# A fused attention and gated-expert kernel: the first loads of k in halves, and the second heads of q on another load queue

## The chip, the cores and the metric

The kernel runs on one core of one Trainium2 chip. The metric is the device time of one execution in microseconds (us), as the median over several runs. A core has a matrix engine (PE, with its weight loads shown apart as PEld), a vector engine (DVE), a scalar engine (ACT), a general engine (POOL, also called GpSimd) and a sync engine (SP) that here only starts transfers. Each engine works through its own instructions in the order in which the program lists them. Transfers between the main memory (HBM) and the on-chip memory are started by SP, ACT and POOL, each with its own queue, and carried by 16 DMA engines that all queues share.

## The reference

Grouped-query attention over 8 batches, 16 query heads, 4 key heads, 384 positions and 64 elements a head, then a two-level gate over 16 experts and the chosen expert's two matrix products for each token.

```
scores = scale * np.matmul(q, k.transpose(0, 1, 3, 2))      # k, v repeated 4 times over heads
attn = softmax(scores)
x = matmul(attn, v)  ->  (3072 tokens, 1024)
g_idx = argmax(x @ w_group);  e_idx = argmax(x @ w_expert[g_idx])
out[token] = g_w * e_w * (relu(x @ w1[g, e]) @ w2[g, e])
```

## The kernel before

The kernel goes through the batches b = 0 to 7. For a batch, attention is cut into NU = 24 units: 4 key heads g (each with its four query heads, held as KG = 2 pairs) times NC = 6 key slices c. The class `Attn` lists the work of a unit: `score(u)` makes four matmuls of q and k into a score tile (L310) and lets ACT take the exponential into a tile e (L316); `pv(u)` multiplies e with v in fp32 (L329); `tail(u)` adds e tiles in pairs on POOL (L336, for c = 1 and 3) and reduces them on DVE (L343) into the softmax's sums. `run` calls `score(u + 2)`, `pv(u)`, `tail(u)` in that order, and after some units the pieces of other work that a table lists by hand (L731 to 745): transposes of q and k, sums, scaling, the gate, the fetch of expert weights. The schedule is manual: the order of the program is the order on each engine. The experts of batch b - 1 (L622, L633) are interleaved with the attention of batch b.

Only the first batch's start is touched here. Before any score can be computed, k and q of batch 0 must be loaded, cast to bf16 and transposed. For later batches this is done by transposing transfers; for batch 0 it is done on PE, with an identity matrix, to be quick:

- SP's queue begins with the first two key heads' rows of k (`k0f[:, 0]`, L157), then the two partition halves of v for key head 0 (`load_v0(0, 1)`, L150), the two halves of v for key heads 1 to 3 (`load_v0(1, Hkv)`, L150 again), the other two heads of k (`k0f[:, 1]`, L173), and v of batch 1 (L107). After these come the transposing transfers of batch 1 (L131, L133, L125), which wait for loads of POOL's queue.
- ACT's queue begins with the two tiles of query heads that key head 0 needs (`q0f[:, 0]` and `q0f[:, 1]`, L159, called q0 and q1 below), then the two gate matrices (L161, L162). ACT then loads its table for the exponential and runs a dummy exponential (L164).
- POOL's queue loads the rest of q of batch 0 with a cast (L170), and k and q of batch 1 (L97, L102).

`first_scores` (L266) orders the start on PE, DVE and ACT. PE runs four small and six large matmuls of ones as filling (L277, L273), DVE casts k (L279), ACT casts q0 (L280), DVE casts q1 (L281). `first_k` transposes the six slices of k twice each (12 transposes, L254) and ACT copies them out to kT (L245). `first_q` transposes q0 and q1 (three each, L262) and DVE copies them out to qT (L247). Two more fillings (L273) follow on PE. Then DVE makes three small index tiles (`index_constants`, L217 to 219), PE computes the first two scores (`at[0].start()`, L676), and `gate_matrix_a` transposes the gate matrices (L225) with two copies on DVE (L227, L231).

Later pieces that the prediction speaks of, all in the first batch or the second: POOL casts the second half of k (`cast_k`, L288) after unit 3 and then adds up v for a guess of the gate (`sum_v`, L467 to 469) after unit 4; DVE makes the inverse sums (L419), spreads them (L426) and scales (L435). PSUM tiles come in two rings, "s" and "o", of two tiles each; "x" is the "o" tile that is not the current one.

Of the kernel before, what the change touches and what calls it, by code (L numbers as in the profile page):

```python
# [18 lines left out]
def kernel(  # L19
# [11 lines left out]
    nc = tc.nc  # L31
    P = 128
    B, Hq, S, D = q.shape
# [7 lines left out]
    KG = KQ // Hkv  # L41
# [3 lines left out]
    H2 = P // 2  # L45
    NC = S // H2
# [22 lines left out]
    def ps_tile(which, shape=None, dtype=F32):  # L69
        if which == "x":  # L70
            which = f"o{1 - turn['o']}"
        else:
            turn[which] = 1 - turn[which]
            which += str(turn[which])
        return psum.tile(shape or [P, 2, 512], dtype, name="ps_" + which)
# [3 lines left out]
    NK = Hkv // 2 * NC  # L79
    k16, qraw, vraw, qT, kT = {}, {}, {}, {}, {}  # L80

    def rows(x):
        return x.rearrange("h (p c) d -> (h p) (c d)", c=NC).rearrange("(a p) n -> p a n", p=P)
# [26 lines left out]
    def new_qT(b):  # L110
        qT[b] = xpool.tile([P, KQ * SC, P], BF16, name="qT")

    def new_kT(b):
        kT[b] = xpool.tile([P, NK, P], BF16, name="kT")
# [26 lines left out]
    q0f = stage[:, :4 * NQ].bitcast(F32).rearrange("p (a n) -> p a n", n=NQ)  # L141
    k0f = stage[:, 4 * NQ:8 * NQ].bitcast(F32).rearrange("p (a n) -> p a n", n=NQ)
# [2 lines left out]
    vraw[0] = vpool.tile([P, Hkv, NC * D], F32, name="v_raw")  # L145
    wraw = stage[:NE // 2 * 5, 16 * NQ:16 * NQ + 2 * Eg * P].bitcast(F32)

    def load_v0(g0, g1):
        for r in range(2):
            nc.sync.dma_start(out=vraw[0][r * H2:(r + 1) * H2, g0:g1],  # L150
                              in_=v[0, g0:g1].rearrange("h (p c) d -> p h (c d)", c=NC))

    onesb = cpool.tile([P, 4 * P], BF16)
    ones1 = cpool.tile([P, P], BF16)
    nc.vector.memset(ones1, 1.0)
    nc.vector.memset(onesb, 1.0)
    nc.sync.dma_start(out=k0f[:, 0], in_=rows(k[0])[:, 0])  # L157
    for m in range(KG):
        nc.scalar.dma_start(out=q0f[:, m], in_=rows(q[0])[:, m])  # L159
    load_v0(0, 1)  # L160
    nc.scalar.dma_start(out=wraw[:KQ], in_=moe_w_group.rearrange("(a p) g -> a (p g)", p=P))  # L161
    nc.scalar.dma_start(out=wraw[KQ:], in_=moe_w_expert.rearrange("g (a p) e -> (g a) (p e)", p=P))  # L162
    early = gpool.tile([P, 1], F32, name="early")
# [5 lines left out]
    for g in range(1, Hkv):  # L169
        nc.gpsimd.dma_start(out=qraw[0][:, KG * g:KG * (g + 1)],  # L170
                            in_=rows(q[0])[:, KG * g:KG * (g + 1)])
    load_v0(1, Hkv)
    nc.sync.dma_start(out=k0f[:, 1], in_=rows(k[0])[:, 1])  # L173
    load_k(1)
# [41 lines left out]
    def index_constants():  # L216
        nc.vector.tensor_copy(out=eidx, in_=eidx_i)  # L217
        nc.vector.tensor_scalar(eback, eidx, -1.0, float(NE - 1), op0=ALU.mult, op1=ALU.add)
        nc.vector.tensor_copy(out=pidx, in_=pback_i)

    def gate_matrix_a():
        pe = ps_tile("o")[:, 0, :Eg * 5 * KQ].rearrange("p (e n) -> p e n", e=Eg)
        wv = wraw.rearrange("a (p e) -> a e p", e=Eg)
        for e in range(Eg):
            nc.tensor.transpose(out=pe[:, e], in_=wv[:, e, :],  # L225
                                identity=id128f[:5 * KQ, :5 * KQ])
        nc.vector.tensor_copy(  # L227
            out=wg[:, :, :NW].rearrange("p k (a e) -> p e a k", e=Eg),
            in_=pe.rearrange("p e (a k) -> p e a k", k=KQ))
        pk = pe.rearrange("p e (a g t) -> p t g a e", a=5, t=KG)[:, 0]  # L230
        nc.vector.tensor_add(out=wgs.rearrange("p g (a e) -> p g a e", e=Eg), in0=pk,  # L231
                             in1=wg[:, 1::2, :NW].rearrange("p g (a e) -> p g a e", e=Eg))
# [10 lines left out]
    def evac(eng, out_, in_):  # L243
        if eng is nc.scalar:
            eng.copy(out=out_, in_=in_)  # L245
        else:
            eng.tensor_copy(out=out_, in_=in_)  # L247

    def first_k(gp, which, eng):
        lo = gp * NC  # L250
        pt = ps_tile(which, [P, 16, P], BF16)
        for i in range(NC):
            for s in range(2):
                nc.tensor.transpose(out=pt[s * D:(s + 1) * D, i, :], in_=k16[0][:, lo + i],  # L254
                                    identity=id128b)
        evac(eng, kT[0][:, lo:lo + NC, :], pt[:, :NC, :])

    def first_q(i0, n, which, eng):
        pt = ps_tile(which, [P, 16, P], BF16)
        for i in range(n):  # L260
            a, c = (i0 + i) // SC, (i0 + i) % SC
            nc.tensor.transpose(out=pt[:, i, :], in_=qraw[0][:, a, c * P:(c + 1) * P],  # L262
                                identity=id128b)
        evac(eng, qT[0][:, i0:i0 + n, :], pt[:, :n, :])

    def first_scores():  # L266
        new_kT(0)
        new_qT(0)
        warm = ps_tile("o")

        def fill(n):
            for i in range(n):
                nc.tensor.matmul(out=warm[:, i % 2, :], lhsT=onesb[:, :P], rhs=onesb, start=True,  # L273
                                 stop=True)

        for i in range(4):
            nc.tensor.matmul(out=warm[:, i % 2, :P], lhsT=ones1, rhs=ones1, start=True, stop=True)  # L277
        fill(6)
        nc.vector.tensor_copy(out=k16[0][:, :NC].rearrange("p c d -> p (c d)"), in_=k0f[:, 0])  # L279
        nc.scalar.copy(out=qraw[0][:, 0], in_=q0f[:, 0])  # L280
        nc.vector.tensor_copy(out=qraw[0][:, 1], in_=q0f[:, 1])  # L281
        first_k(0, "s", nc.scalar)
        first_q(0, SC, "s", nc.vector)
        first_q(SC, SC, "o", nc.vector)
        fill(2)

    def cast_k():
        nc.gpsimd.tensor_copy(out=k16[0][:, NC:NK].rearrange("p c d -> p (c d)"), in_=k0f[:, 1])  # L288
# [378 lines left out]
    def do(f, *a):  # L667
        return lambda: f(*a)

    gate_constants()
    first_scores()
    index_constants()
    at = {0: Attn(0), 1: Attn(1)}
    at[0].start()  # L676
    gate_matrix_a()
    state, weights = {}, {}

    new_qT(1)  # L680
# [45 lines left out]
    def second_scale():  # L726
# [7 lines left out]
        4: [gate_matrix_b, do(sum_v, 0, nc.gpsimd)],  # L734
        6: [do(collect, 0, 0, 1)],
        7: [do(first_q, 2 * GB, 2 * GB, "x", nc.vector)],
        8: [do(first_k, 1, "x", nc.vector)],
        10: [do(sums, 0, 0, 1, "x"), do(normalise, 0, 0)],
        13: [first_guess],
        14: [do(cast, 0, 0)],  # L740
# [20 lines left out]
    pt = ps_tile("x")  # L761
# [125 lines left out]
    for c in range(SC):  # L887
# [5 lines left out]
        for i, (n0, n1) in enumerate(parts):  # L893
# [8 lines left out]
            for j, (ps, x) in enumerate(halves(c)):  # L902
                eng = nc.scalar if j and i % 2 == 0 else nc.sync
# [5 lines left out]
    with tc.For_i(0, n_left, 1):  # L909
# [27 lines left out]
        x = xb[B]  # L937
        w1, w2 = fetch1(er), fetch2(er)
        m = gpool.tile([P, B, SC, NE], F32, name="pm")
# [51 lines left out]
```

The softmax here doesn't subtract the row's maximum and nothing guards it: scores larger than these inputs give would overflow.

## Time and profile before

| | before |
|---|---|
| median of 4 runs | 367.02 us (366.3 to 367.65) |
| the profiled execution, its own time | 367.06 us |
| its span, first to last instruction | 365.4 us |
| PE busy | 353.5 us, 97% of the span |
| DVE busy | 275.9 us, 75% |
| ACT busy | 229.9 us, 63% |
| POOL busy | 160.2 us, 44% |
| first score matmul on PE | 7.15 us into the span |
| first exponential on ACT | 7.56 us |
| first expert matmul (L622) | 49.50 us |

Times inside the span are counted from its first instruction. A line of the timeline gives the start, the busy time, the engine, the line of the program, the operation, what is written and read, and in brackets the idle time before it with what ended it. The chain of waits follows the work that ended last back from the end, at each step to what released it. A matmul's end in the trace is modelled, so PE's busy share says little about how close it is to its peak. A transfer's time to landing runs from its issue to the moment at which its completion is seen.

In the first 49.5 us PE is idle for about two us in all, in a few places; after that the trace shows waits of PE of at most 0.5 us in any one place, and 0.9 us in all.

### The profile page before, as it was taken

The page shows a single profiled execution, that of the slowest core. Times are in us where ns is not written, and L with a number is a line of the kernel's source. Part 1 is how long each engine was busy: PE and PEld are TensorE (multiplying, and loading weights), DVE is VectorE, ACT ScalarE, POOL GpSimd, SP SyncE. Part 2 cuts the span into 40 slices and gives each one's busy share as a digit, 9 for nine tenths or more (in the row PEclk, how much of TensorE's full clock was granted, in tenths as well). Part 3 has the DMA queues.
Part 4 walks back from the last instruction along what each step waited for, and adds up shares of the span by engine and source line. Part 5 has one row for each costly group of instructions (what it writes and reads, how often), then busy time and mean ns, then how long its engine had stood idle before and what let it go on. Part 6 is the DMA issues. An engine that isn't in the chain of part 4 may idle for free.

```text
span 365.4 us, 9409 instructions
## 1 busy us (share of the span) xinstructions
PE 353.5 (97%) x3892; PEld 183.2 (50%) x3907; DVE 275.9 (75%) x506; ACT 229.9 (63%) x300; POOL 160.2 (44%) x127
## 2 busy tenths in 40 slices
PE   8999899999999999999999999999999999999992
PEld 3544455445455454554555455554445545555641
DVE  5689998858988498867989579884998659882230
ACT  4889853759926597367954599265972579544221
POOL 6887890736802376043730377131760258300000
PEclk9999999999999999999999999999999999999998
DMA  8974999999999999999997999999999599998333
GB/s 192 241 119 69 188 189 221 148 217 252 223 164 194 231 248 209 144 192 269 230 198 156 208 265 212 155 198 228 250 208 150 95 256 237 213 212 191 87 74 104
DMA packets 69902, 69.79 MB, mean 191 GB/s; under 512 B 35832, under 2 KB 49944, under 8 KB 69856
## 3 DMA queue, kind: packets, MB, share of 16 engines
q0 software_dynamic: 26864, 41.81, 64.9%
q1 hardware_dynamic: 42320, 26.40, 31.2%
q10 hardware_dynamic: 672, 0.93, 0.8%
q8 instruction: 32, 0.52, 0.6%
q14 instruction: 14, 0.11, 0.1%
HBM read 89.21 MB, written 12.58 MB: 279 GB/s over the span
## 4 chain that ended last, share of the span: by engine, by line
PE 85%; POOL 5%; DVE 3%; issue 3%; ACT 1%; DMA 1%; POOLq 0%; ACTq 0%
PE ps_o L329 27%; PE ps_s L622 22%; PE ps_s L633 13%; PE ps_s L310 7%; PE ps_o L633 7%; PE ps_o L451 3%; POOL e L336 3%; PE ps_s L896 2%; PE ps_o L622 1%; PE ps_o L896 1%; DMA w<-in_q_dram 1%; DVE red L343 1%; ACT e L316 1%; PE ps_o L415 1%; POOL xT L435 1%
## 5 line engine op out<-in xcount | busy, mean ns | idle before, releaser
L316 ACT ACTIVATE e<-ps_s 128x768 f32<-128x768 f32 x192 | 150.6, 815 | 19.8 <-PE ps_s L310 16.1
L329 PE MATMUL ps_o<-e,v_raw 64*64 64x384 f32 x1536 | 153.3, 483 | 0.7 <-DVE inv L419 0.6
L336 POOL TENSOR_TENSOR e<-e 128x768 f32<-128x768 f32 x64 | 116.5, 1838 | 70.4 <-ACT e L316 51.3
L343 DVE TRANSPOSE_TENSOR_REDUCE red<-e 128x24 f32<-128x768 f32 x128 | 114.1, 946 | 17.6 <-POOL e L336 17.5
L622 PE MATMUL ps_s<-xb,w 128*128 128x384 bf16 x480 | 81.0, 326 | 0.5 <-ACT e L316 0.5
L329 PEld LDWEIGHTS ps_o<-e,v_raw 64*64 64x64 f32 x1536 | 55.4, 133 | 38.9 <-issue 27.4
L622 PEld LDWEIGHTS <-w 128*128 128x128 bf16 x512 | 48.9, 98 | 36.2 <-issue 4.7
L310 PE MATMUL ps_s<-qT,kT 64*64 64x384 bf16 x768 | 63.7, 326 | 0.7 <-ACT e L316 0.2
L626 ACT ACTIVATE hT<-ps_s 128x768 bf16<-128x768 f32 x30 | 24.3, 811 | 61.0 <-PE ps_s L622 58.0
L633 PE MATMUL ps_s<-w,hT 128*128 128x512 bf16 x211 | 49.0, 379 | 0.9 <-issue 0.2
L633 PEld LDWEIGHTS <-hT 128*128 128x128 bf16 x336 | 31.2, 97 | 36.7 <-issue 2.1
L310 PEld LDWEIGHTS <-kT 64*64 64x64 bf16 x768 | 24.1, 105 | 39.2 <-issue 37.4
L426 DVE STREAM_TRANSPOSE rb<-inv 128x384 f32<-128x384 f32 x62 | 32.0, 555 | 0.4
L689 POOL COPY after<-qT 128x1 bf16<-128x1 bf16 x7 | 1.7, 244 | 69.8 <-DMA qT<-q_raw 68.4
L658 ACT ACTIVATE ot<-ps_s,we 128x1024 f32<-128x1024 f32 x14 | 15.6, 1115 | 25.5 <-PE ps_o L489 12.0
L633 PE MATMUL ps_o<-w,hT 128*128 128x512 bf16 x111 | 26.3, 379 | 0.1
L435 DVE TENSOR_TENSOR xT<-xT,rb 128x768 f32<-128x768 f32 x25 | 24.0, 959 | 0.9
L245 ACT CAST xb<-xT 128x768 bf16<-128x768 f32 x27 | 21.7, 830 | 0.0
L461 DVE TENSOR_REDUCE vsum<-v_raw 128x256 bf16<-128x1536 f32 x6 | 16.9, 2815 | 0.0
L379 DVE COPY xT<-ps_o 128x768 f32<-128x768 f32 x18 | 16.6, 920 | 0.0
L660 DVE TENSOR_SCALAR ot<-ps_o,we 128x1024 f32<-128x1024 f32 x7 | 9.0, 1282 | 5.6 <-PE ps_o L633 5.6
L560 POOL DMA_DIRECT2D w<-in_moe_w_dram x8 | 7.3, 917 | 11.9 <-PE ps_s L310 9.3
(129 smaller groups left out, 202.6 us busy)
## 6 DMA issues: line engine op xcount, KB each, us to landing
w<-in_moe_w_dram POOLq DMA_DIRECT2D x16, 2048.0 KB, 23.8
out_dram<-ot SPq DMA_DIRECT2D x42, 256.0 KB, 6.6
q_raw<-in_q_dram POOLq DMA_DIRECT2D x7, 768.0 KB, 31.7
v_raw<-in_v_dram SPq DMA_DIRECT2D x12, 384.0 KB, 4.9
k<-in_k_dram POOLq DMA_DIRECT2D x7, 192.0 KB, 28.4
out_dram<-ot SPq DMA_DIRECT2D x7, 128.0 KB, 2.3
v_raw<-in_v_dram POOLq DMA_DIRECT2D x2, 384.0 KB, 11.6
w<-in_q_dram POOLq DMA_DIRECT2D x3, 192.0 KB, 6.9
```

Of the source, the lines that this page charges most:

```text
L245: eng.copy(out=out_, in_=in_)
L310: nc.tensor.matmul(out=sT[r * H2:(r + 1) * H2, s, :S], lhsT=kT[b][s * D:(s + 1) * D, slot, ks], rhs=qT[b][s * D:(s + 1) * D, kq * SC:(kq + ...
L316: nc.scalar.activation(e.rearrange("p t (s x) -> p s t x", s=2), sT[:, :, :S].rearrange("p s (t x) -> p s t x", t=2), ACT.Exp, scale=scale)
L329: nc.tensor.matmul(out=oT[t * D:(t + 1) * D, r, :S], lhsT=vraw[b][r * H2:(r + 1) * H2, g, c * D:(c + 1) * D], rhs=self.e[u][r * H2:(r + 1) ...
L336: eng.tensor_add(out=self.e[u], in0=self.e[u], in1=self.e[u + 1])
L343: nc.vector.tensor_reduce(out=reds[self.b][:, g, n].rearrange("p t j -> p (t j)"), in_=self.e[u].rearrange("p t (j x) -> p (t j) x", x=32) ...
L426: nc.vector.transpose(out=rb[:, r].rearrange("p (j x) -> p j x", x=32), in_=inv[b][:, 2 * m + r].unsqueeze(2).to_broadcast([P, NB, 32]))
L435: eng.tensor_mul(out=x, in0=x, in1=rb)
L461: eng.tensor_reduce(out=vsum[b], in_=vraw[b].rearrange("p g (c d) -> p g d c", d=D), axis=AX.X, op=ALU.add)
L622: nc.tensor.matmul(out=h[:, jj, :S], lhsT=w1[:, kq, (f0 + jj) * P:(f0 + jj + 1) * P], rhs=x[:, kq, :], start=(kq == 0), stop=(kq == KQ - 1))
L626: nc.scalar.activation(hT[:, f0:f0 + 2, :], h[:, :, :S], ACT.Relu)
L633: nc.tensor.matmul(out=y[:, nh, :], lhsT=hT[:, f, c * P:(c + 1) * P], rhs=w2[:, f, nh * HALF:(nh + 1) * HALF], start=(f == 0), stop=(f == ...
```

## The change

The load of the first two heads of k is cut into two transfers, one for slices 0 to 2 (KA = 3) and one for slices 3 to 5. SP's queue now begins with the first half of k, then q1 (before: ACT's second load), then the second partition half of v's head 0, then the second half of k. ACT's queue has q0, then the first partition half of v's head 0, then the gate matrices. The cast of k, its transposes and the copy to kT come in halves too. The first half stays where it was, ahead of q. The second half's cast is the last thing that `first_scores` gives to DVE; its six transposes come on PE after the first two scores, and DVE copies them out (before: ACT, with the first half). One more filling matmul stands on PE between the transposes of q0 and of q1. `index_constants` moves behind `gate_matrix_a` on DVE. Since one more tile of the "o" ring is taken, the roles of its two tiles swap from there on.

```diff
-    def load_v0(g0, g1):
+    def load_v0(g0, g1, engs=(nc.sync, nc.sync)):
         for r in range(2):
-            nc.sync.dma_start(out=vraw[0][r * H2:(r + 1) * H2, g0:g1],
+            engs[r].dma_start(out=vraw[0][r * H2:(r + 1) * H2, g0:g1],
                               in_=v[0, g0:g1].rearrange("h (p c) d -> p h (c d)", c=NC))
...
-    nc.sync.dma_start(out=k0f[:, 0], in_=rows(k[0])[:, 0])
-    for m in range(KG):
-        nc.scalar.dma_start(out=q0f[:, m], in_=rows(q[0])[:, m])
-    load_v0(0, 1)
+    KA = NC // 2
+
+    def load_k0(n0, n1):
+        nc.sync.dma_start(out=k0f[:, 0, n0 * D:n1 * D], in_=rows(k[0])[:, 0, n0 * D:n1 * D])
+
+    load_k0(0, KA)
+    for m, eng in enumerate((nc.scalar, nc.sync)):
+        eng.dma_start(out=q0f[:, m], in_=rows(q[0])[:, m])
+    load_v0(0, 1, (nc.scalar, nc.sync))
+    load_k0(KA, NC)
...
-    def first_k(gp, which, eng):
-        lo = gp * NC
+    def first_k(n0, n1, which, eng):
         pt = ps_tile(which, [P, 16, P], BF16)
-        for i in range(NC):
+        n = n1 - n0
+        for i in range(n):
             for s in range(2):
-                nc.tensor.transpose(out=pt[s * D:(s + 1) * D, i, :], in_=k16[0][:, lo + i],
+                nc.tensor.transpose(out=pt[s * D:(s + 1) * D, i, :], in_=k16[0][:, n0 + i],
                                     identity=id128b)
-        evac(eng, kT[0][:, lo:lo + NC, :], pt[:, :NC, :])
+        evac(eng, kT[0][:, n0:n1, :], pt[:, :n, :])
...
         fill(6)
-        nc.vector.tensor_copy(out=k16[0][:, :NC].rearrange("p c d -> p (c d)"), in_=k0f[:, 0])
+        cast_k0(0, KA)
         nc.scalar.copy(out=qraw[0][:, 0], in_=q0f[:, 0])
         nc.vector.tensor_copy(out=qraw[0][:, 1], in_=q0f[:, 1])
-        first_k(0, "s", nc.scalar)
+        first_k(0, KA, "s", nc.scalar)
         first_q(0, SC, "s", nc.vector)
+        fill(1)
         first_q(SC, SC, "o", nc.vector)
         fill(2)
+        cast_k0(KA, NC)
+
+    def cast_k0(n0, n1):
+        nc.vector.tensor_copy(out=k16[0][:, n0:n1].rearrange("p c d -> p (c d)"),
+                              in_=k0f[:, 0, n0 * D:n1 * D])
...
     first_scores()
-    index_constants()
     at = {0: Attn(0), 1: Attn(1)}
     at[0].start()
+    first_k(KA, NC, "o", nc.vector)
     gate_matrix_a()
+    index_constants()
...
-        8: [do(first_k, 1, "x", nc.vector)],
+        8: [do(first_k, NC, NK, "x", nc.vector)],
```

## The prediction

> **What bounds the kernel now.** I read the page first: PE is busy 97% of the span, and the list of PE's waits after 49.5 us holds 0.9 us in all. So whatever moves the first expert matmul (49.50 us) moves the end one for one, and only the stretch before it can absorb or pass on anything. I therefore read the chain of waits in order of time for the first 10 us, then the timeline up to 50 us.
>
> The chain of waits at the start (start, duration, what):
>
> ```profile
> 1.33 3.71 DMA w<-in_q_dram
> 5.07 0.80 DVE w L281
> 5.91 0.50 PE ps_o L262 x3
> 6.41 0.81 PE ps_o L273 x2
> 7.22 0.32 PE ps_s L310 x4
> 7.56 0.82 ACT e L316
> 8.38 0.04 issue
> 8.42 0.36 PE ps_s L310 x4
> ```
>
> The reader is to see that the first score waits for the landing of q1 (issued 1.33, landed 5.04), its cast, its transposes and then two fillings. k is not in this chain. It landed 3.0 us after its issue at 0.88, so at 3.88, and PE took up its transposes at 4.41, when the six fillings were through.
>
> But PE's start isn't what reaches 49.5 us. The timeline further on:
>
> ```profile
> 11.79 1.82 POOL L336 TENSOR_TENSOR e<-e 128x768 f32<-128x768 f32 x1 [0.36 <-PE ps_s L310]
> 13.90 0.51 POOL L288 CAST w<-w 128x384 bf16<-128x384 f32 x1 [0.29 <-DMA w<-in_k_dram]
> ...
> 17.77 3.60 POOL L336 TENSOR_TENSOR e<-e 128x768 f32<-128x768 f32 x2
> ...
> 19.63 1.84 DVE L343 TRANSPOSE_TENSOR_REDUCE red<-e 128x24 f32<-128x768 f32 x2 [0.55 <-POOL e L336]
> ...
> 38.40 0.42 PE L415 MATMUL ps_o<-rsum,half 128*64 128x24 f32 x8 [0.92 <-DVE rsum L405]
> ...
> 48.64 1.52 ACT L316 ACTIVATE e<-ps_s 128x768 f32<-128x768 f32 x2 [0.84 <-POOL e L336]
> ...
> 49.50 2.76 PE L622 MATMUL ps_s<-xb,w 128*128 128x384 bf16 x16 [0.55 <-ACT e L316]
> ```
>
> POOL stands 0.29 us at L288 until the other heads of k (k1, L173) land at about 13.87. From there it is busy through v's sums (L467 to 469) to the add at 17.77; DVE waits 0.55 us for that add at 19.63 and is then busy for nearly all of 20 to 36 us (3.93, 3.79, 3.83 and 3.97 of each 4 us); PE waits for DVE at 38.40, DVE and POOL hand over to each other until 48.6, and ACT and PE wait for POOL. So a gain of PE at 7 us ends in longer waits, while a shift of **k1's landing** goes through POOL, DVE and POOL to 49.5 and to the end.
>
> **The change, part by part.** I work it against the profiled execution: 367.06 us, of which 365.4 are span and 1.66 lie around it. The median, 367.02, stands 0.04 below.
>
> ACT's queue: q1's issue (432 ns, median of L159) gives way to half of v (588 ns, median of L150), +0.16 us. Table load, dummy exponential and the cast of q0 on the same engine are behind it: the cast ends at 4.88 rather than 4.72.
>
> PE up to q0: the first half of k is 6 transposes where 12 took 0.85 us, so 0.43; 4.41 + 0.43 = 4.84. q0's transposes then start with the cast, at about 4.93 (before: 5.19), and need about 0.32 before the next matmul. The added filling takes 0.41 (0.81 for two in the chain): PE is free for q1 at 5.66.
>
> q1's landing. It is issued on SP where v was, at 1.35, as early as on ACT. Ahead of or beside it are now half of k and q0. The trace has no such order, so bounds: at best it lands as q0 does, 4.08 (issue 0.88 plus 3.2); at worst like the first v load that stood in this place of SP's queue, 1.35 + 4.1 = 5.45. Bytes say earlier than 5.04, since 96 KB of k leave its front; I take 4.6, midway between q0 and q1 of before. Its cast takes 0.36 (L279) to 0.78 (L281), so it ends at 4.96 to 5.38, ahead of 5.66. The transposes start at 5.66 rather than 5.91, and the same 1.31 us lead to the first score: 6.97, a gain of 0.25. Bounds: 5.45 + 0.78 gives 6.29, a loss of 0.38; and no landing is worth more than 0.25, as PE is the limit there.
>
> A rule speaks against any gain: the Trainium skill, DMA: Bandwidth & Descriptors, section "Issuing engines are not separate DMA queues", says that loads from different engines share the same 16 DMA engines and that spreading them only saves issue time. By it q1 would stay at 5.04 and the gain above would be nothing, which leaves the end where the next paragraphs put it.
>
> PE after the first scores: six transposes are inserted before the gate's. Six warm ones took 0.51 (L262 at 10.16), half of twelve 0.43. I take 0.43. They lie in the wait for the first exponential, but that wait has only 8.42 - 8.27 = 0.15 us left behind the gate's transposes, so 0.28 comes on the path of PE. Together PE stands at 0.28 - 0.25 = +0.03 from the second score on: nothing. Bounds: -0.1 to +0.7. Even +0.7 would be mostly covered, as the adds on POOL would end at 14.3 rather than 13.61, against k1's landing at 13.87.
>
> The second half of k: its load ends about as v's second load did before (1.93 + 4.7 = 6.6), as the same bytes are ahead of both. DVE's cast of it is queued behind q's last copy (ended 6.80), and only gate copies and index tiles stand behind it, so a wait there of up to 0.5 us costs nothing; PE reaches its transposes at about 7.4. The copy to kT leaves ACT (half of 0.80) for DVE, before unit 3's score; ACT was idle 1.46 us there, DVE 0.95. `index_constants` (0.69 in sum) move in time on an idle DVE and are first read at 28 us. All nothing. If the second half landed after 7.2, PE would stand still for the excess.
>
> SP's queue: seven loads instead of six up to k1, one more issue of 0.4 to 0.6. SP:
>
> ```profile
> 1.35 3.35 SPq L150 DMA_DIRECT2D v_raw<-in_v_dram  x4
> 4.75 0.74 SPq L173 DMA_DIRECT2D w<-in_k_dram  x1
> 5.54 1.41 SPq L107 DMA_DIRECT2D v_raw<-in_v_dram  x2
> ```
>
> k1 is issued at 4.75 and lands 9.1 us later, so an issue 0.5 later is covered by its queue's backlog. What counts is what is ahead of it. Before, SP's queue held 192 (k) + 192 + 576 (v) + 192 (k1) = 1152 KB, 1.18 MB, and had moved 0.25 MB by 4.0 us: 0.93 MB left for 9.87 us, 0.094 MB a us. After, it holds 1248 KB, 1.28 MB. If by 4.0 it has moved half of the 0.64 MB that both hardware queues moved before, 0.96 is left: +0.3 us. If it moved 0.39, as ACT's queue did, 0.89: -0.4. And if the second half of k, 128 short packets, costs as much as 128 whole ones, 0.098 MB more counts: +0.3 + 1.0 = +1.3. The rows of 4.0 to 13.9 lie between:
>
> ```profile
> q0 software_dynamic: 1288, 0.94, 65.6%
> q1 hardware_dynamic: 908, 1.26, 48.7%
> ```
>
> 65.6% of 16 x 9.9 us over 1288 packets is 81 ns for 730 bytes; 48.7% over 908 is 85 ns for 1390 bytes. That is the packet's price rather than the byte's, but POOL's loads cast, which SP's don't. I take +0.45, near the bytes.
>
> The Trainium skill, DMA: Bandwidth & Descriptors, section "Queues, rings and completion order", has each DMA engine go round its queues by whole packets; no row here shows the order within an engine. By that alone the packet's price would hold, and the sum would be 368.4.
>
> v's heads 1 to 3 (last landing 4.11 + 8.3 = 12.4) are needed by unit 6 at 14.5; 1.3 later is still covered.
>
> **Sum.** PE 0, POOL's chain +0.45: 367.06 + 0.45 = **367.5 us**. With the ends -0.4 and +1.3, less or more 0.3 for run and rounding: 366.5 to 368.1 as this case's own range. What a measurement of this kernel can tell from no change is about 0.3%, 1.1 us, so this is no change, leaning to a loss.
>
> **Rivals.**
>
> *Slower, by k1's place in SP's queue.* The short packets and the longer queue cost by packets. For it: the two rows above, and that k1 landed long after the queue's average, with load of batch 1 already moved. Against it: 96 KB of extra queue only. It decides from a landing at 15.0 on: +1.3 to +1.6 gives 368.5.
>
> *Slower, by the start.* q1 at 5.45 or the second half of k after 8 us holds PE in order, and the filling adds 0.41 with nothing to hide it; 0.38 + 0.28 and a stop of 0.8 on PE make 1.5 in excess of POOL's 0.29 wait: 1.2 net, 368.3. Against it: the bytes ahead are not more.
>
> *Faster.* k1 lands 0.4 earlier and POOL's adds don't wait; that is capped by the adds at 13.61 less 0.25, so 0.5 us. Beyond it there is one larger piece on the DVE chain: L580 at 28.50 takes 1.62 us where its neighbours of the same size take 0.17 to 0.23, beside POOL's add from 28.27 to 30.09. An add that starts 0.25 later against DVE would free 1.4. Then 367.06 - 0.4 - 1.2 = 365.5. Against it: that add starts from a matmul which itself waits for DVE, so both shift together.
>
> *The change does nothing:* q1 lands as before and k1 too, 367.1; it lies within the forecast.
>
> **How the numbers follow.** Forecast 0.42, k1's queue 0.28, the start 0.12, faster 0.18. So slower by over 0.3% has 0.40, the same 0.42, faster 0.18. To leave no more than 2 in 10 out, the range takes in most of both: 365.6 to 368.8.
>
> **What would show it.** Right: q1's transposes near 5.7 and the first score near 7.0; L288 on POOL starting later than 13.90, and the first L622 later than 49.50 by the same amount. Wrong: L288 starting at POOL's adds with no wait, or a first L622 that moves with the first score and not with k1; a loss of over 1.1 us without a later L288; or a changed L580.

## The result, and the profile after

The changed kernel takes 367.57 us (median of 51 runs, 366.94 to 369.87) against 367.00 for the kernel before (78 runs): ratio 1.0015, interval 1.0009 to 1.0021. That is a small loss, clear of noise and inside the 0.3% called no change. The profiled execution took 367.29 us, with a span of 365.6 us, against 367.06 and 365.4. (All line numbers from here on that stand beside the changed kernel are its own: the scores are L322, POOL's cast L300, its sums of v from L479, the first expert matmul L634.)

The chain of waits of the changed kernel in order of time (start, duration, what):

```profile
...
2.42 5.26 DMA w<-in_k_dram
7.68 0.02 issue
7.71 0.27 DVE w L296
7.98 0.04 issue
8.02 0.36 PE ps_o L260 x6
8.38 0.60 PE ps_o L231 x4
8.98 0.29 PE ps_s L322 x4
...
```

q1 is gone from the start of the chain; the second half of k has taken its place. It is issued at 2.42 and lands at 7.68. The timeline of the changed kernel:

```profile
5.72 0.33 PE L268 MATMUL ps_o<-id128b,w 128*128 128x128 bf16 x3
5.89 0.59 PE L279 MATMUL ps_o<-onesb 128*128 128x512 bf16 x2
6.41 0.60 PE L322 MATMUL ps_s<-qT,kT 64*64 64x384 bf16 x8
...
8.02 0.36 PE L260 MATMUL ps_o<-id128b,w 128*64 128x128 bf16 x6 [1.01 <-DVE w L296]
...
8.91 0.36 PE L322 MATMUL ps_s<-qT,kT 64*64 64x384 bf16 x4
...
12.28 1.83 POOL L348 TENSOR_TENSOR e<-e 128x768 f32<-128x768 f32 x1 [0.33 <-PE ps_s L322]
14.05 0.51 POOL L300 CAST w<-w 128x384 bf16<-128x384 f32 x1
...
49.83 2.44 PE L634 MATMUL ps_s<-xb,w 128*128 128x384 bf16 x14 [0.54 <-ACT e L328]
```

The reader is to see a start that is 0.74 us earlier (first score 6.41 instead of 7.15; how much of this belongs to the change is taken up below) and is then lost: PE stands 1.01 us at the six transposes of the late half, and the second pair of scores comes at 8.91 instead of 8.42. POOL's second add starts at 12.28 instead of 11.79, its cast of the other heads of k at 14.05 instead of 13.90, and the first expert matmul at 49.83 instead of 49.50.

The load of those other heads of k, k1, is issued later (timeline of SP's issues in the changed kernel; 4.75 before):

```profile
5.26 0.74 SPq L179 DMA_DIRECT2D w<-in_k_dram  x1
```

In this execution it landed 8.5 us later, at 13.78, before POOL came to it, and so it ended no wait here. The experiments show that this is not so in every execution.

### The profile page after: what moved, and what is told of

The parts are those of the page before. It is cut to its first block, busy times and chain, and to the rows that moved or that the text cites. A ratio compares the mean times of both kernels' runs of the same rounds, so it can differ in the third digit from the quotient of the medians.

```text
span 365.6 us, 9415 instructions
## 1 busy us (share of the span) xinstructions
PE 353.0 (97%) x3893; PEld 183.5 (50%) x3908; DVE 276.2 (76%) x508; ACT 229.5 (63%) x300; POOL 159.8 (44%) x127
## 4 chain that ended last, share of the span: by engine, by line
PE 85%; DVE 5%; POOL 3%; ACT 2%; DMA 1%; issue 1%; SPq 0%; POOLq 0%; ACTq 0%
PE ps_o L341 27%; PE ps_s L634 22%; PE ps_s L645 13%; PE ps_s L322 7%; PE ps_o L645 7%; PE ps_o L463 3%; DVE red L355 3%; POOL e L348 2%; PE ps_s L909 2%; ACT e L328 1%; DMA w<-in_k_dram 1%; PE ps_o L634 1%; PE ps_o L909 1%; PE ps_o L427 1%; DVE rb L438 1%
## 5 line engine op out<-in xcount | busy, mean ns | idle before, releaser
L634 PE MATMUL ps_s<-xb,w 128*128 128x384 bf16 x480 | 81.0, 326 | 0.5 <-ACT e L328 0.5
L634 PEld LDWEIGHTS <-w 128*128 128x128 bf16 x512 | 48.9, 98 | 36.2 <-issue 4.7
L322 PE MATMUL ps_s<-qT,kT 64*64 64x384 bf16 x768 | 63.8, 326 | 0.5 <-ACT e L328 0.2
L322 PEld LDWEIGHTS <-kT 64*64 64x64 bf16 x768 | 24.4, 105 | 39.0 <-issue 37.2
```

Source lines behind the costliest of these rows:

```text
L322: nc.tensor.matmul(out=sT[r * H2:(r + 1) * H2, s, :S], lhsT=kT[b][s * D:(s + 1) * D, slot, ks], rhs=qT[b][s * D:(s + 1) * D, kq * SC:(kq + ...
L634: nc.tensor.matmul(out=h[:, jj, :S], lhsT=w1[:, kq, (f0 + jj) * P:(f0 + jj + 1) * P], rhs=x[:, kq, :], start=(kq == 0), stop=(kq == KQ - 1))
```

## The experiments

All ratios are against the kernel before, run on the same chip beside them, with a 95% interval in brackets; they are not the quotients of the medians that are given. Each profile is of one execution.

**Second half of k ahead of v on SP.**

```diff
-    load_v0(0, 1, (nc.scalar, nc.sync))
     load_k0(KA, NC)
+    load_v0(0, 1, (nc.scalar, nc.sync))
```

> As the changed kernel, but with the second half of k ahead of v's second partition half in SP's queue. Theory A (the changed kernel loses because PE stops 1.0 us in order for the late second half of k, landing 7.68): the half lands by about 6.6, PE's wait ahead of its transposes falls from 1.01 to under 0.2 us, the second pair of scores starts near 8.1 instead of 8.91, POOL's cast of the other heads of k near 13.8, the first expert matmul near 49.5 instead of 49.83; ratio to the kernel before 0.999 to 1.000. Rival B (the one load more on SP and its short packets cost, wherever they stand): no change against the changed kernel, ratio 1.0010 to 1.0020. Rival C (v landing later now stops PE or POOL instead): v's half lands near 7.7, covered until the first product with v at about 8.2, so at most +0.1.

Measured: 367.46 us, ratio 1.0015 (1.0002 to 1.0028). The half landed at 6.8, PE's wait fell to 0.46, the second pair of scores started at 8.00. But POOL's cast started at 14.00, after a wait of 0.81 for k1, and the first expert matmul at 49.58. So PE got nearly all its time back, and the loss stayed. Theory A alone falls, if narrowly: its upper end, 1.000, lies just below the interval.

**One load for k, halves only in the compute.**

```diff
-    load_k0(0, KA)
+    load_k0(0, NC)
...
-    load_k0(KA, NC)
```

> As the changed kernel, but k's first two heads in one load again; casts and transposes stay in halves, q's second tile stays on SP. Theory A: k lands near 3.9 and nothing stops PE; q's second tile lands near 5.0, the first score near 6.8; second pair of scores near 8.2; ratio 0.9985 to 1.000. Rival B: the same, since the extra load is gone too. Rival D (the inserted transposes behind the first scores are what costs, whatever the load): ratio stays at 1.001 to 1.002.

Measured: 367.72 us, ratio 1.0036 (1.0015 to 1.0058). A miss for every theory as stated: the load that stopped PE was a new one. The gate matrices, behind half of v on ACT's queue, landed near 8.3, and PE waited 0.77 for them at 8.43; the second pair of scores came at 9.00, the first expert matmul at 49.92.

**Only the queues changed.** The kernel before with q1 second on SP and half of v on ACT.

> The kernel before with only the queues changed: q's second tile second on SP, one half of v on ACT. Theory A: q's second tile lands within 0.3 of 5.04, first score within 0.3 of 7.15, first expert matmul at 49.4 to 49.6; ratio 0.9990 to 1.0005. Rival E (the move of the loads lets q land sooner by itself): first score at 6.5 or earlier, and if PE's start reached the end, ratio 0.998.

Measured: 369.61 us, ratio 1.0062 (1.0036 to 1.0087). q1 landed at 5.05, against 5.04 on ACT. The gate matrices landed near 8.6 and PE waited 1.57 for them. In the profiled execution (370.04 us) PE's clock then fell. Windows of that execution (stretch; busy time and, in brackets, the number of instructions for PE, PEld, DVE, ACT, POOL; then the granted PE clock, the DMA share and GB/s):

```profile
7.00:8.80 1.80, 0.23 (x7) 0.05 (x1) 0.20 (x1) 1.51 (x2) 0.00 (x0) 1.00 1.26 206
8.80:10.00 1.20, 1.20 (x12) 0.99 (x16) 0.47 (x2) 0.03 (x1) 0.00 (x0) 0.62 1.21 259
10.00:11.00 1.00, 1.00 (x12) 0.20 (x8) 0.20 (x1) 0.78 (x1) 0.00 (x0) 0.50 1.20 275
11.00:12.50 1.50, 1.50 (x16) 0.46 (x8) 0.00 (x0) 0.81 (x1) 1.11 (x1) 0.50 1.19 276
```

PE was busy for 0.23 of 1.8 us; then the clock was 0.62 and 0.50 until 12.5, and a score matmul took 524 ns instead of 323. The first expert matmul came at 51.84. q1's landing was as theory A had it; the times and the ratio failed for both, as neither had the gate matrices in it.

**POOL's sums of v later, in the kernel before.**

```diff
-        4: [gate_matrix_b, do(sum_v, 0, nc.gpsimd)],
+        4: [gate_matrix_b],
+        9: [do(sum_v, 0, nc.gpsimd)],
```

> The kernel before with POOL's sums of v (3.4 us) listed after unit 9 instead of unit 4, so that the adds of the second head come first. If POOL's chain from its cast of k through these sums to the add at 17.77 sets the end, as the prediction says: the add starts near 16.2, DVE's wait of 0.55 at 19.63 goes, the inverse sums at 21.39 come 0.4 to 0.5 sooner, the first expert matmul near 49.0, ratio 0.9985 to 0.9990. If PE's pace sets it: ratio 0.9997 to 1.0003.

Measured: 367.37 us, ratio 1.0015 (1.0003 to 1.0028); the inverse sums came 1.29 earlier, at 20.10, but at 23.26 PE's weight load had waited 1.46 for the sums of v themselves, and its matmuls stood for 0.80. The first expert matmul came at 49.27. The move made a new wait, so this run does not say whether POOL's chain sets the end.

**Late loads needed later.** The changed kernel with the second half's transposes after unit 0 and the gate's after unit 2.

```diff
-        pe = ps_tile("o")[:, 0, :Eg * 5 * KQ].rearrange("p (e n) -> p e n", e=Eg)
+        pe = ps_tile("x")[:, 0, :Eg * 5 * KQ].rearrange("p (e n) -> p e n", e=Eg)
...
-    first_k(KA, NC, "o", nc.vector)
-    gate_matrix_a()
...
+        0: [do(first_k, KA, NC, "x", nc.vector)],
         1: [do(first_q, GB, GB, "x", nc.vector)],
+        2: [gate_matrix_a],
```

> As the changed kernel with its loads unchanged, but PE needs the late ones later: the second half of k's transposes come after unit 0 and the gate matrices' after unit 2, instead of ahead of the second pair of scores. Theory A (the loss is PE's stop, in order, for the second half of k or the gate matrices): the second pair of scores starts when the first exponential is through, at 7.7 to 8.0 instead of 8.91; POOL's cast of the other heads of k then waits again for its load and starts at 13.7 to 13.9; first expert matmul at 49.3 to 49.5; ratio 0.9985 to 1.0000. Rival B (the loads themselves, one more and shorter packets, delay what is needed later): loads unchanged, so first expert matmul stays at 49.8 and the ratio at 1.001 to 1.002.

Measured: 367.99 us, ratio 1.0036 (1.0021 to 1.0051). The second pair of scores did start at 8.10, but the next one waited 0.46 for the copy to kT, POOL's second add came at 12.41, and k1 landed at 14.67: POOL's cast started at 14.72, the first expert matmul at 50.48. A miss for theory A, and slower than rival B had it as well.

**Only q1 on SP, halved transposes.** ACT has q0 and the gate matrices; k is one load.

```diff
-    load_k0(0, KA)
+    load_k0(0, NC)
...
-    load_v0(0, 1, (nc.scalar, nc.sync))
-    load_k0(KA, NC)
+    load_v0(0, 1)
```

> The changed kernel with k's first two heads in one load and both halves of v back on SP behind q's second tile, so that ACT's queue is q's first tile and then the gate matrices; of the change in the loads only q's second tile on SP is left. If it was v on ACT's queue that made the gate matrices late in the runs with one k load (landing 8.3 and 8.6, PE waiting 0.8 and 1.6): they land near 5.5, PE does not wait for them, the second pair of scores starts at 8.1 to 8.4 and the ratio is 0.9995 to 1.0005 instead of 1.0036. If SP's longer queue or the halved transposes cost it: ratio stays above 1.002.

Measured: 367.12 us, ratio 1.0001 (0.9990 to 1.0011). PE waited for no load between 5 and 16 us, the second pair of scores came at 7.45, and k1 was issued at 4.70 and landed at 13.43. PE was 0.97 ahead of the kernel before, POOL waited 0.84 for k1, and the first expert matmul came at 49.09. The second of the gate matrices landed at 5.69 here and at 8.30 in the kernel with one load for k, which differs from this one in half of v on ACT alone. So that half made it late there. It is not all that can: in the other profiles it landed at 6.7 to 8.7 with half of v on ACT and at 6.1 to 7.5 without.

**Only the compute order, loads of the kernel before.**

> The loads of the kernel before with the compute order of the changed one: cast and transposes of k in halves, second half behind the first scores, one more filling, index tiles later. The prediction's sum for PE: 0.28 lost behind the first scores, nothing gained ahead of them as q's second tile lands as before; nothing of it reaches the end since POOL waits 0.29 for k: ratio 0.9995 to 1.0005. If the inserted transposes and filling cost of themselves: 1.001 or more.

Measured: 366.97 us, ratio 1.0003 (0.9987 to 1.0019). From the first to the second pair of scores it took 1.40 us (6.79 to 8.19) against 1.27 before; POOL waited 0.59 for k1 and its cast started at 13.97. No loss is shown for the halved transposes and the filling.

**Second half of k on ACT, v on SP.**

```diff
-    def load_k0(n0, n1):
-        nc.sync.dma_start(out=k0f[:, 0, n0 * D:n1 * D], in_=rows(k[0])[:, 0, n0 * D:n1 * D])
+    def load_k0(n0, n1, eng=nc.sync):
+        eng.dma_start(out=k0f[:, 0, n0 * D:n1 * D], in_=rows(k[0])[:, 0, n0 * D:n1 * D])
...
-    load_v0(0, 1, (nc.scalar, nc.sync))
-    load_k0(KA, NC)
+    load_k0(KA, NC, nc.scalar)
+    load_v0(0, 1)
```

> As the changed kernel, but the second half of k is ACT's second load and both halves of v's first head are SP's third and fourth. Theory A: the second half lands near 4.9 to 5.5, the gate matrices near 6.5 to 7, v near 7; nothing stops PE after the first score at 6.4, the second pair of scores starts at 7.7 to 8.0; then only the landing of the other heads of k near 13.8 limits; ratio 0.9985 to 1.0000. Rival B: 1.001 to 1.002 as in the changed kernel.

Measured: 367.52 us, ratio 1.0008 (0.9999 to 1.0017), between the two expectations and with an interval that reaches both, so the ratio decides nothing here. The timeline of this kernel:

```profile
7.47 0.36 PE L322 MATMUL ps_s<-qT,kT 64*64 64x384 bf16 x4
...
14.65 0.51 POOL L300 CAST w<-w 128x384 bf16<-128x384 f32 x1 [1.99 <-DMA w<-in_k_dram]
...
20.36 1.84 DVE L355 TRANSPOSE_TENSOR_REDUCE red<-e 128x24 f32<-128x768 f32 x2 [2.22 <-POOL e L348]
...
22.45 0.88 PE L341 MATMUL ps_o<-e,v_raw 64*64 64x384 f32 x8 [1.73 <-DVE inv L431]
...
50.23 1.95 PE L634 MATMUL ps_s<-xb,w 128*128 128x384 bf16 x11 [0.54 <-ACT e L328]
```

This is the clearest single profile of the study. Nothing stops PE, and it is 0.95 us ahead of the kernel before. k1 was issued at 5.41 and landed 9.2 later; POOL waits 1.99 us, DVE waits 2.22 for POOL, PE waits 1.73 for DVE, and the first expert matmul comes 0.73 later than in the profile before.

**What the profiles have in common.** POOL's start is the start of its cast of k1, or of its sums of v where these come first (last four rows). Times in us.

| kernel | second pair of scores | POOL's wait for k1 | POOL's start | first expert matmul | difference |
|---|---|---|---|---|---|
| before | 8.42 | 0.29 | 13.90 | 49.50 | 35.60 |
| changed | 8.91 | 0 | 14.05 | 49.83 | 35.78 |
| second half of k ahead of v | 8.00 | 0.81 | 14.00 | 49.58 | 35.58 |
| one load for k | 9.00 | 0 | 14.14 | 49.92 | 35.78 |
| only the queues | 9.38 | 0 | 16.04 | 51.84 | 35.80 |
| late loads needed later | 8.10 | 0.49 | 14.72 | 50.48 | 35.76 |
| only q1 on SP | 7.45 | 0.84 | 13.49 | 49.09 | 35.60 |
| only the compute order | 8.19 | 0.59 | 13.97 | 49.54 | 35.57 |
| second half of k on ACT | 7.47 | 1.99 | 14.65 | 50.23 | 35.58 |
| before, swapped | 8.17 | - | 13.32 | 49.11 | 35.79 |
| changed, swapped | 9.23 | - | 14.39 | 50.16 | 35.77 |
| second half of k on ACT, swapped | 8.07 | - | 13.22 | 49.00 | 35.78 |
| only q1 on SP, swapped | 8.02 | - | 13.17 | 48.94 | 35.77 |

Over a range of 2.9 us the difference stays within 0.23. Two rows say most: with only q1 on SP and with the second half of k on ACT, PE is at the second pair at 7.45 and 7.47, but POOL starts at 13.49 and 14.65, and the first expert matmul follows POOL, at 49.09 and 50.23. So POOL's start sets the first expert matmul, and it is the later of two things: the landing of k1 and the end of POOL's second add, which PE's pace sets.

A row by itself is one execution, and PE's own start differs between executions of the same start. The kernel with the sums of v later begins as the kernel before does, and yet its second pair came at 7.77, not 8.42, and its first expert matmul at 49.27. The second half of k on ACT had its second pair at 7.47, and at 8.07 with the swap that follows, which does not touch the start. So a lead of PE in one row is not by itself the work of that kernel's loads.

k1 was issued at 5.18 to 5.41 in the four unswapped kernels with two loads for k's first heads, and landed at 13.78, 13.94, 14.60 and 14.67 (mean 14.25). In the six with one load, the sums of v later among them, it was issued at 4.64 to 4.87 and landed at 13.24 to 14.04 (mean 13.64). The two ranges of landings overlap.

What makes the issue late isn't the length of k1's own queue. In the next two pairs of lines k1 is SP's seventh load both times, first with only q1 on SP, then with the second half of k on ACT:

```profile
1.80 2.85 SPq L150 DMA_DIRECT2D v_raw<-in_v_dram  x4
4.70 0.69 SPq L178 DMA_DIRECT2D w<-in_k_dram  x1
...
1.80 3.57 SPq L150 DMA_DIRECT2D v_raw<-in_v_dram  x4
5.41 0.64 SPq L179 DMA_DIRECT2D w<-in_k_dram  x1
```

In every one of the 14 traces SP waits for a landing once before it issues k1, and always at the ninth load of SP's and ACT's queues, counted together in the order of the program. The releaser that the trace names is the landing of q0 (here the changed kernel: waited in total, times, longest, in us):

```profile
SPq L150 <- DMA w<-in_q_dram: 0.7, 1, 0.7
```

With ten loads on the two queues up to k1 the ninth is v's last (issued at 4.11 in the kernel before), and k1 alone stands behind it. With eleven the ninth is v's last but one (3.73 in the changed kernel), and one more issue of some 0.7 stands between the wait and k1, on whichever queue the load was added.

**The swap** takes k1's landing out: POOL's cast of k1 goes behind its sums of v, in four kernels.

```diff
-        3: [cast_k],
-        4: [gate_matrix_b, do(sum_v, 0, nc.gpsimd)],
+        4: [gate_matrix_b, do(sum_v, 0, nc.gpsimd), cast_k],
```

> The kernel before with POOL's cast of the other heads of k moved behind its sums of v, so that POOL's chain no longer starts at that load's landing. Theory (in nine profiles the first expert matmul came 35.6 to 35.8 us after POOL began that cast, and the cast began at the later of two times: the load's landing and the end of POOL's second add): the sums start with the add's end, 13.6 instead of 14.37, so 0.3 to 0.8 us are gained until PE's pace or v's landing limits; first expert matmul at 48.9 to 49.3; ratio 0.9980 to 0.9992. If the time of that landing does not matter: 0.9997 to 1.0003.

Measured: 366.71 us, ratio 0.9980 (0.9958 to 1.0001). The sums start at 13.32 with no wait; first expert matmul 49.11. Its start is that of the kernel before, but in this execution PE was early (first score 6.02) and then stood 0.98 for the gate matrices, which landed at 7.47:

```profile
7.60 0.64 PE L225 MATMUL ps_o<-id128f,w 40*128 40x40 f32 x4 [0.98 <-DMA w<-in_moe_w_expert_dram]
```

> The changed kernel with the same swap on POOL. If the landing of the other heads of k (0.5 later issued, behind one load more) is what costs the changed kernel its time, the swap takes its loss away: the same ratio as the kernel before with the swap, within 0.0005. If PE's stop for the late second half of k is what costs it, POOL's second add still ends at 14.1 and the loss against the swapped kernel before stays: 0.5 us, ratio higher by 0.0010 to 0.0018.

Measured: 367.33 us, ratio 1.0013 (0.9992 to 1.0034), so 0.62 more than the swapped kernel before, by medians of 12 runs each; seven of its runs lie above all twelve of that kernel. In its profile PE stands 1.04 at the late half:

```profile
8.34 0.36 PE L260 MATMUL ps_o<-id128b,w 128*64 128x128 bf16 x6 [1.04 <-DVE w L296]
...
14.39 1.81 POOL L479 TENSOR_TENSOR rb<-v_raw 128x768 f32<-128x768 f32 x1
```

With k1 out of the way the late half still costs.

> Second half of k second on ACT's queue, and the swap on POOL. Without the swap its PE was 0.95 us ahead of the kernel before at the second pair of scores and POOL stood 1.99 us waiting for the other heads of k. With the swap the second add ends near 12.7 and the sums of v start near 12.8 (v lands near 12.4 to 13.5): PE's lead reaches the end; first expert matmul at 48.4 to 48.9; ratio 0.9970 to 0.9985. If the lead at PE's start is worth nothing, 0.9990 as the swapped kernel before.

Measured: 366.29 us, ratio 0.9980 (0.9961 to 0.9998), the lowest median of all, and 0.42 below the swapped kernel before. Its interval lies below the kernel before, but the gain over the swapped one is not clear of noise. All its twelve runs (366.95 at most) lie below all twelve of the changed kernel swapped (367.06 at least), from which it differs in one thing: the second half of k has changed queues with half of v. In its profiled execution PE's lead was small (second pair 8.07), the sums started at 13.22 and the first expert matmul at 49.00, not the 48.4 to 48.9 expected.

> One load for k, q's second tile second on SP, both halves of v behind it, halved transposes, and the swap on POOL. Second pair of scores near 7.5 (0.95 ahead of before); first expert matmul at 48.4 to 48.9; ratio 0.9970 to 0.9985, as with the second half of k on ACT.

Measured: 366.91 us, ratio 0.9993 (0.9975 to 1.0011), short of what was expected; in its profile q1 landed only at about 5.2, and the second pair came at 8.02.

So two things hold the changed kernel back, the late half and the late k1: with the late half cured and k1 late (second half on ACT) 367.52; with k1 out of the way and the half late (changed, swapped) 367.33; with both cured 366.29. That the late half costs is clear of noise. For k1 alone the ratio of 1.0008 is not; there the profile shows the chain, and the swap, which took 0.45 off the kernel before, turned 0.57 above the kernel before into 0.87 below it (medians of the runs beside each other).

## Why the prediction was right, point by point

The time was right, 367.5 against 367.57, and so was the bound: what moves POOL's cast of k1 moves the end. Its term of +0.45 for k1 is of the right size: +0.6 by the means above. That the sum comes out so near is in part luck all the same. It had PE at nothing and all of the loss in k1. In the changed kernel's profile k1 landed no later than before (13.78 against 13.85), and POOL's cast came straight behind its add, with no wait, which the prediction had named as a sign of being wrong. What made POOL late there was PE's stop for the second half of k, which the sum had at nothing. The two do not add up: POOL starts at the later of them, so the one hides the other. Nor did the first expert matmul move "by the same amount" as POOL's cast: 0.33 against 0.15 (the last point has what goes with it). PE's idle time ahead of the first expert matmul was 4.1 us in the kernel before, 1.2 of it ahead of the first matmul, and not about two; no step below uses it.

- **q1's landing, its transposes.** 4.6 and 5.66 were said; 1.35 + 3.3 = 4.65 and 5.72 measured. The landing is right. The 5.72 is right by two errors that cancel. ACT's cast of q0 started 0.45 later than before (4.67 against 4.22), not 0.16, as ACT's issue of the first gate matrix took 0.98 us instead of 0.62; so q0's transposes came at 5.22, not 4.93. They and the filling then took 0.50 instead of 0.73. That the move to SP wins nothing by itself agrees: 5.05 with the queues alone. The share of the gain that is due to the halved load is not settled, as q1 landed at 4.65 with one load for k as well.
- **The first score**, 6.97 said, 6.41 measured. (6.97 counts from the chain's 7.22; from the timeline's 7.15 it would be 6.90.) The step that the same 1.31 us, 1.24 on the timeline, lead from q1's transposes to the score failed: it took 0.69, since the two fillings took 0.59 together instead of 1.02. One filling had 634 ns at the slowest and 379 ns at the fastest in the same profile; the kernel before never got below 594. This is a matter of when PE speeds up, not of the change: the two kernels that begin exactly as the kernel before have 6.50 (sums of v later) and 6.02 (swapped).
- **PE behind the first scores**, 0.28 lost: 0.06 to 0.15 where PE waited for no load (1.33 to 1.42 against 1.27). Mis-sized; the inserted transposes lie mostly under the first exponential.
- **The second half of k**, "ends about as v's second load did before ... 6.6": this step failed. It landed at 7.68, and near 8.0 and 7.75 in the two other profiles with that queue order. The argument was that the same bytes are ahead of both; measured, 5.26 us from issue to landing where v's load took 4.7, and issued at 2.42 rather than 1.97. What followed from a late landing was put rightly, "PE would stand still for the excess", and stood as a rival at 0.12: it cost PE 1.01 us. Without any delay of k1 it costs 0.62, by the two swapped kernels.
- **k1 in SP's queue**, "an issue 0.5 later is covered by its queue's backlog. What counts is what is ahead of it": the reverse was measured. From issue to landing it took 8.5 to 9.5 us with two loads and 8.5 to 9.4 with one; on the mean the landing followed the issue, 0.61 later for an issue 0.54 later. That the issue would be 0.5 later was right in size; its reason, "seven loads instead of six" on SP, was not: with only q1 on SP there are seven too, and k1 is issued at 4.70. It is the count over both queues, as above. The price of short packets, and with it the 368.4 by the rule on packets, isn't needed; no run separates packets from bytes.
- **The gate matrices** on ACT's queue were counted only as ACT's own delay (+0.16). Behind half of v they were late enough to stop PE for 0.77 and 1.57 us as soon as the second half of k did not stop it first, and with the loads of the kernel before they stopped it for 0.98 in one execution in which PE was early. In the changed kernel PE reached them after they had landed. The prediction did not see it.
- **The faster rival's large piece**, that DVE's L580 might be freed of 1.4 us: no run frees it. With the late loads needed later the same instruction (L592 there) took 0.23 instead of 1.62, but the next one took 1.74 instead of 0.18:

```profile
29.30 0.23 DVE L592 TENSOR_SCALAR oh_all<-key,km 128x16 f32<-128x16 f32 x1
29.57 1.74 DVE L595 SCALAR_TENSOR_TENSOR t<-eidx,oh_all 128x16 f32<-128x16 f32 x1
```

In all 14 profiles one of these two instructions ends within 0.1 us of the end of POOL's add beside it, and so the time moves with that add. It took 1.61 or 1.62 us in the five rows of the table with a difference of 35.57 to 35.60, and 1.74 to 1.84 in the eight with 35.76 to 35.80; with it go the 0.2 between the two groups and the 0.2 between the 0.15 and the 0.33 above. What freeing it would win stays open.

## What to carry to other kernels

When the trace has a chain that starts at one engine's first wait, predict that start: it is the later of a landing and of the engine's own backlog, and curing one shows only the other. A load cut in two is one more issue. Look for the place at which the issuing engine waits for an earlier landing, and count the loads of all its neighbours up to there: here one more load on either of two queues put one more issue behind that wait, and every load after it moved by that issue. Before a transfer is put ahead of another, look up what stands in order behind the one that becomes late, in the program order of the engine that reads it.

## What the runs showed of the hardware that was not expected

PE's speed at the start differed from one profile to the next: the same filling took 634 ns or 379 ns, with the first of 379 at 5.50 us in the changed kernel and none up to the last filling at 6.6 in the kernel before, while the granted clock in the windows read 1.00 from the start. A pause of PE of 1.8 us with 0.23 us of work in it was followed by about 3.4 us at a granted clock of 0.50: narrower windows of the same execution read 1.00 up to 9.0, 0.75 from 9.0 to 9.2, 0.50 from there to 12.4, 0.72 from 12.4 to 12.6 and then 1.00. Stops of 0.77 to 1.04 in four other profiles were followed by 1.00 up to 15 us. The Trainium skill, TensorE: Matmul & The Clock Gate, part 1 on the clock gate, gives a free-running window of about 3.4 us after which PE's rate doubles or halves; the stretch at half rate agrees with that length, and the granted clock of 1.00 beside fillings of 634 ns does not show the slow start.
